# Last pass of a two-layer attention backward: V and its dS product two blocks further ahead of K, and wo read row by row

## The chip, the cores and the metric

The kernel runs on one core of a Trainium2 chip. The metric is the device time of one execution in microseconds. Three runs of the kernel before took 2030.9, 2032.97 and 2034.32 us; the median is 2032.97 us. The engines are named as in the profile: PE is TensorE (PEld are its weight loads), DVE is VectorE, ACT is ScalarE, POOL is GpSimd and SP is SyncE. A "q" behind an engine's name is its queue of DMA issues.

## The reference

A token (one row of 1024 numbers) goes through attention, a dense layer, the same attention once more and the same dense layer once more; then the gradients of everything are taken. Both attentions use one K cache and one V cache of 4 groups x 65536 rows x 128 numbers in bf16, that is 64 MiB each, and their gradients are as large.

```python
def _A_ref(x, k_cache, v_cache, wq, wo):
    q = (x @ wq).reshape(B, Sq, Hq, Dh)...        # 32 heads of 128
    k = jnp.repeat(k_cache, rep, axis=1)          # 4 groups, 8 heads each
    v = jnp.repeat(v_cache, rep, axis=1)
    scores = jnp.einsum("bhqd,bhkd->bhqk", q, k) * (Dh ** -0.5)
    o = jnp.einsum("bhqk,bhkd->bhqd", _softmax(scores, axis=-1), v)
    return o... @ wo
...
x = x + _A_ref(_layernorm(x), A_k_cache, A_v_cache, A_wq, A_wo)
x = x + _B_ref(_layernorm(x), B_w1, B_b1, B_w2, B_b2)
x = x + _A_ref(_layernorm(x), A_k_cache, A_v_cache, A_wq, A_wo)
x = x + _B_ref(_layernorm(x), B_w1, B_b1, B_w2, B_b2)
```

The outputs are the last x and the gradients of x, K, V, wq, wo, w1, b1, w2 and b2.

## The kernel before

**Four passes over K and V.** Pass 1 and pass 2 are the two forward attentions, pass 3 is the backward of the second attention and pass 4, the last, the backward of the first. Pass 4 also writes dK and dV, for both attentions at once: what a layer adds to dK and dV is an outer product of a column of the softmax and its gradient with a row of q or dO, so the 8 heads of both layers (16 rows) go into one product. Between the passes lie dense stages with w1, w2, wo and wq.

**Columns, items, blocks.** The 65536 rows of a group lie as 512 columns of 128 rows. A pipeline item is 8 columns; a block is J = 32 columns, four items, 1 MiB of K or of V. Pass 4 has 256 items, 64 blocks.

**The pipeline.** `pipeline` (L788) steps through the items; at step i a stage with lag l works on item i - l. In pass 4 (L1367) the stages are: `vT`, lag 0, transposes V on TensorE and evacuates it to `kt` (L1267); `vS`, lag 2, multiplies the transposed V by dO into one PSUM bank `ps_sc` (L1308) and, after four items, VectorE multiplies this dP by the kept exponentials E into `X` (L1316), which is dS; `dV8`, lag 3, makes dV of a block by outer products (L1329); `k8`, lag 7, multiplies K by X for dQ (L1355) and makes dK by outer products. The outer products need E and X transposed; that is `x_transpose` (L1285), of E at `vS`'s first item of a block, from a copy `xin` that POOL makes at `vT` (L1282), and of X right after X is made (L1318).

**Space.** The arena is one tile of 20 granules of 8 KiB a partition. Twelve (`NSLOT`) are for blocks of K and V, weight slabs, and staging of dV, dK and the weight gradients. The other eight are the planes of E, one for each layer and group; the planes of group g are granules 12+g and 16+g. When a group is done, its two planes become free for loads (`E_done`, L836). In pass 4 a block's granule is chosen in `take_one` (L279), and the groups run from 3 to 0. Seven blocks of V that pass 3 has turned already stay in the arena for the start of pass 4.

**Order.** Passes 1 to 3 keep the written order on PE, DVE and ACT. In pass 4 the framework's scheduler orders each engine's instructions beforehand from its own model of time; on the chip each engine then runs its list in order, and waits on semaphores. Loads are issued on SP, stores on POOL, each queue in its order. So a load whose granule is still being stored holds up the loads behind it on SP.

**Background work.** Between the items run generators, a step at a time (`Background`, L725): the projections by wq (`g_q`), by wo (`g_wo`, L859), the products of wo with the gradient (`g_dO`, L903) and wq's (`g_dn`, L930), and in pass 4 the weight gradients (`g_outer`, L1397, and `g_outer_wide`, L1416). A slab of wo for one group is 1024 x 1024, 2 MiB. In the passes it is read by `wo_runs` (L465): each partition gets eight neighbouring rows of wo, 8 or 16 KiB in one piece. Since a partition then holds other rows than the head's vector does, small matmuls with constants (`to_runs`, `from_runs`, `eighth`) turn the vector beforehand or the result afterwards. For the slabs at the ends of the passes, `wo_slabs` (L461) reads row by row: 2 KiB pieces, with the rows where the vectors have them. wq is always read in pieces of 2 KiB (`wq_slabs`, L457).

Of the kernel before, what the change touches and what calls it, by code (L numbers as in the profile page):

```python
# [10 lines left out]
BF = mybir.dt.bfloat16  # L11
# [5 lines left out]
P = 128  # L17
# [3 lines left out]
def kernel(  # L21
# [35 lines left out]
    J = 32  # L57
# [69 lines left out]

    eighth = const.tile([P, 8], F32, name="eighth")
    nc.vector.tensor_reduce(out=eighth[:], in_=ident_f[:].rearrange("p (m e) -> p e m", e=8), axis=AX.X, op=ALU.add)
    sixt = const.tile([P, 16], F32, name="sixt")  # L130
    nc.vector.tensor_reduce(out=sixt[:], in_=ident_f[:].rearrange("p (m e) -> p m e", e=8), axis=AX.X, op=ALU.add)
    to_runs = const.tile([P, 8, 16], BF, name="to_runs")
    nc.vector.tensor_copy(out=to_runs[:, :, :], in_=sixt[:, :].unsqueeze(1).to_broadcast([P, 8, 16]))
    sixt2 = const.tile([P, 16], F32, name="sixt2")
    nc.vector.tensor_reduce(out=sixt2[:], in_=ident_f[:].rearrange("p (a m) -> p m a", m=16), axis=AX.X, op=ALU.add)
    from_runs = const.tile([P, 16, 8], F32, name="from_runs")
    nc.vector.tensor_copy(out=from_runs[:, :, :], in_=sixt2[:, :].unsqueeze(2).to_broadcast([P, 16, 8]))


# [37 lines left out]
    def col_from_dram_f(v1d, n, name):  # L177
        nj = n // P
        rows = tmp.tile([nj // 4, 4 * P], BF, name="rows_f", tag="rows_f", bufs=1)
        nc.sync.dma_start(out=rows[:], in_=v1d.rearrange("(s x) -> s x", x=4 * P))  # L180
        pt = ps_mv([P, 4, 8], BF)
        col = vec.tile([P, nj // 4, 4], F32, name=name)
        for j in range(4):
            nc.tensor.transpose(pt[:, j, 0:nj // 4], f_cols(rows, j), ident_b[0:nj // 4, 0:nj // 4])
            nc.vector.tensor_copy(out=col[:, :, j], in_=pt[:, j, 0:nj // 4])
        return col[:, :, :].rearrange("p s j -> p (s j)")

    def col_to_dram_f(col, n, v1d):
        nj = n // P
        rows = tmp.tile([nj // 4, P, 4], BF, name="rows_f", tag="rows_f", bufs=1)  # L190
        c3 = col[:, :].rearrange("p (s j) -> p s j", j=4)
        for j in range(4):
            pt = ps_mv([nj // 4, P], F32)
            nc.tensor.transpose(pt[:, :], c3[:, :, j], ident_f[:, :])
            nc.vector.tensor_copy(out=rows[:, :, j], in_=pt[:])
        nc.gpsimd.dma_start(out=v1d.rearrange("(s x) -> s x", x=4 * P), in_=rows[:].rearrange("s p j -> s (p j)"))

# [188 lines left out]
    B3_LAG = TLEAD + HB // 8 + 3  # L386
    B4_LAG = TLEAD + J // 8 + 1
    DV_LAG = TLEAD + 1
    ITEMS = [order_by_unit(False, SU), order_by_unit(True, SU), order_by_unit(False, HB), order_by_unit(True, J)]
# [71 lines left out]
    def wo_slabs(g, ahead=1):  # L461
        v = rows_of(A_wo)
        return slabs("s_wo", lambda k, kn: v[:, g * R + k:g * R + k + kn, :], R, 4, 1024, ahead, True)

    def wo_runs(g):  # L465

        v = A_wo[g * 1024:(g + 1) * 1024, :].rearrange("(p k) n -> p k n", k=8)
        return slabs("s_wo", lambda k, kn: v[:, k:k + kn, :], R, 4, 1024, 1, True)[0]

# [389 lines left out]
    def g_wo(L, xacc, g, ps=ps_bg, it=None):  # L859
        def fin(p):  # L860
            nc.vector.tensor_tensor(out=xacc[:], in0=xacc[:], in1=p, op=ALU.add)
        if it is not None:
            yield from g_mv(it, R, 8, lambda kc: L["oTb"][:, g * R + kc:g * R + kc + 1], ps, fin)
            return
        each = tmp.tile([P, R, 8], BF, name="run_each", bufs=1)
        nc.vector.tensor_tensor(out=each[:, :, :], in0=L["oTb"][:, gsl(g)].unsqueeze(2).to_broadcast([P, R, 8]),
                                in1=eighth[:, :].unsqueeze(1).to_broadcast([P, R, 8]), op=ALU.mult)
        yield
        pt = ps_mv([P, R, 8])
        nc.tensor.matmul(pt[:, :, :].rearrange("p r k -> p (r k)"), lhsT=to_runs[:, :, :].rearrange("p a b -> p (a b)"),  # L870
                         rhs=each[:, :, :].rearrange("p r k -> p (r k)"), start=True, stop=True)
        yield
        own = tmp.tile([P, 8, R], F32, name="run_own", bufs=1)
        nc.vector.tensor_tensor(out=own[:, :, :], in0=pt[:, :, :].rearrange("p r k -> p k r"),
                                in1=M8[:, :].unsqueeze(1).to_broadcast([P, 8, R]), op=ALU.mult)
        oruns = tmp.tile([P, 8], F32, name="run_o")
        nc.vector.tensor_reduce(out=oruns[:], in_=own[:, :, :], axis=AX.X, op=ALU.add)
        orunb = tmp.tile([P, 8], BF, name="run_ob")
        nc.vector.tensor_copy(out=orunb[:], in_=oruns[:])
        yield  # L880
        yield from g_mv(wo_runs(g), R, 8, lambda kc: orunb[:, kc:kc + 1], ps, fin)

# [20 lines left out]
    def g_dO(L, dx, g):  # L903
        def fin(y):
            each = tmp.tile([P, R, 8], F32, name="run_own", bufs=1)
            nc.vector.tensor_tensor(out=each[:, :, :], in0=y.unsqueeze(1).to_broadcast([P, R, 8]),
                                    in1=M8[:, :].unsqueeze(2).to_broadcast([P, R, 8]), op=ALU.mult)
            yield
            pt = ps_mv([P, R, 8], F32)
            nc.tensor.matmul(pt[:, :, :].rearrange("p r k -> p (r k)"), lhsT=from_runs[:, :, :].rearrange("p a b -> p (a b)"),  # L910
                             rhs=each[:, :, :].rearrange("p r k -> p (r k)"), start=True, stop=True)
            yield
            own = tmp.tile([P, R, 8], F32, name="run_own", bufs=1)
            nc.vector.tensor_tensor(out=own[:, :, :], in0=pt[:, :, :], in1=eighth[:, :].unsqueeze(1).to_broadcast([P, R, 8]), op=ALU.mult)
            back = tmp.tile([P, R], F32, name="run_o")
            nc.vector.tensor_reduce(out=back[:], in_=own[:, :, :], axis=AX.X, op=ALU.add)
            yield
            yield from dO_finish(L, g)(back[:, :])
        yield from g_rowdots(wo_runs(g), R, dx[:], DC, fin, "%s_dO%d" % (L["name"], g))

# [17 lines left out]
    def attn_fwd(p, L, on_group, bg, end=()):  # L938
# [56 lines left out]
        def stats(g, su, S, pm):  # L995
# [23 lines left out]
            def low():  # L1019
                gm = tmp.tile([R, 1], F32, name="gm")  # L1020
                nc.vector.tensor_reduce(out=gm[:], in_=v["ptm"][:], axis=AX.X, op=ALU.min)
                v["gmb"] = tmp.tile([R, P], F32, name="gmb", bufs=1)
                nc.vector.tensor_scalar(out=v["gmb"][:], in0=ones_f[0:R, :], scalar1=gm[:, 0:1], scalar2=None, op0=ALU.mult)
# [194 lines left out]
    def attn_bwd4(p, La, Lb, on_group, bg, stack, end=()):  # L1218
# [48 lines left out]
        def vT(g, c8):  # L1267
            bg.need(g)
            vb8 = kv8("v", g, c8)
            if is_turned("v", g, c8):  # L1270
                state[("vt", g, c8)] = vb8
            else:
                pt = ps_tr()
                for i in range(8):
                    nc.tensor.transpose(pt[:, i, :], vb8[:, i, :], ident_b[:, :])  # L1275
                kv_done("v", g, c8)
                vt = turned_to("v", g, c8, vb8)
                evac(vt[:, :, :], pt[:, :, :])
                state[("vt", g, c8)] = vt
            if c8 % J == 0:  # L1280
                xin = dspool.tile([P, J, R2], BF, name="xin", tag="xin", bufs=1)
                nc.gpsimd.tensor_copy(out=split2(xin[:, :, :]), in_=E2(g, c8, J))  # L1282
                state[("xin", g, c8 // J)] = xin

# [8 lines left out]
        def vS(g, c8):  # L1293
            if c8 == gfirst[g]:
                g_setup(g)
            if c8 == sufirst[(g, c8 // SU)]:
                su_setup(g, c8 // SU)
            if c8 % J == 0:
                state[("xe", g, c8 // J)] = x_transpose(state.pop(("xin", g, c8 // J)))
            vt = state.pop(("vt", g, c8))  # L1300
# [11 lines left out]
            if (c8 + 8) % J == 0:  # L1312
                c0 = c8 + 8 - J
                ps_dp = state["ps_dp"]
                X = dspool.tile([P, J, R2], BF, name="X", tag="X")
                nc.vector.tensor_tensor(out=split2(X[:, :, :]), in0=split2(ps_dp[:, :, :]), in1=E2(g, c0, J), op=ALU.mult)  # L1316
                add_load(dve=0.13 + J * R2 * 0.00105)
                state[("xd", g, c0 // J)] = (X, x_transpose(X[:, :, :]))  # L1318
                E_done(g, c0, J)

# [22 lines left out]
        def k8(g, c8):  # L1343
            kb8 = kv8("k", g, c8)
            b, j0 = divmod(c8, J)
            su = c8 // SU
            X, xt = state[("xd", g, b)]
            if c8 == sufirst[(g, su)]:
# [17 lines left out]
        start_pass(p)  # L1366
        pipeline(items, [(vT, 0), (vS, TLEAD), (dV8, DV_LAG), (k8, B4_LAG)], bg, end)  # L1367

# [333 lines left out]
```

## Time and profile before

The profiled execution took 2032.97 us; its span from first to last instruction is 2031.2 us.

| | value |
|---|---|
| profiled execution, time | 2032.97 us |
| its span | 2031.2 us |
| PE busy / PEld / DVE / ACT / POOL | 81% / 66% / 58% / 51% / 7% |
| HBM read, written | 624.96 MB, 165.69 MB |
| mean rate over the span | 389 GB/s |
| first product of the last pass with V (L1308) | 1229.5 us |
| a load of 1 MiB of V or K, issue to landing | 15.0 and 14.6 us |
| a store of 1 MiB, issue to landing | 11.8 us |

The page has the busy share of each engine, then 40 slices of the span with the busy tenths, the granted TensorE clock and the rate of the DMA engines, then the DMA queues, the chain of work that ended last, and groups of instructions by line with what ended the idle time before them. Waits are inferred from semaphore events; where several were awaited, the last one is named. A busy TensorE includes modelled ends of its instructions, so "busy" is not "at its peak". Times in windows count from the span's start.

### The profile page before, as it was taken

What the parts mean: (1) busy time and instruction counts of PE and PEld (TensorE: products, weight loads), DVE (VectorE), ACT (ScalarE), POOL (GpSimd) and SP (SyncE); (2) the same over time, 40 slices, a digit from 0 to 9 for tenths busy, and PEclk for the clock granted to TensorE, in tenths of its full rate; (3) what the DMA queues carried; (4) which work ended last, traced back from release to release, by engine and by line L of the source; (5) the groups of instructions that cost most, each with busy time, mean ns of one, the idle gap of its engine ahead of it and who ended that gap; (6) DMA issues with size and microseconds to landing.
All of it is one profiled execution on the core that took longest, in us unless ns stands there. A gap on an engine that the chain in (4) does not pass through costs nothing. (4 is left out here: it accounts for less than half of the span.)

```text
span 2031.2 us, 67119 instructions
## 1 busy us (share of the span) xinstructions
PE 1646.9 (81%) x30228; PEld 1345.0 (66%) x30228; DVE 1178.5 (58%) x2409; ACT 1043.9 (51%) x1609; POOL 142.2 (7%) x332
## 2 busy tenths in 40 slices
PE   6877787787877877788787897798797887788996
PEld 6877777687777776777777795455455555455554
DVE  5645455345555544535454466587577676677666
ACT  3434354143443453426354265586476676567665
POOL 0000000000000000000000001111011111111111
PEclk9989999699999998988898998798699789899777
DMA  9999999989999998899999976999999999899985
GB/s 391 421 424 421 423 424 400 379 343 421 424 421 423 425 401 313 360 421 416 419 422 413 391 273 263 356 418 423 419 381 423 394 418 419 332 422 425 424 339 228
DMA packets 101006, 794.98 MB, mean 391 GB/s; under 512 B 9440, under 2 KB 9454, under 8 KB 37102
## 3 DMA queue, kind: packets, MB, share of 16 engines
q1 hardware_dynamic: 76670, 624.99, 75.1%
q0 software_dynamic: 24048, 165.70, 19.7%
q8 instruction: 236, 3.87, 0.7%
q14 instruction: 52, 0.43, 0.1%
HBM read 624.96 MB, written 165.69 MB: 389 GB/s over the span
## 5 line engine op out<-in xcount | busy, mean ns | idle before, releaser
L164 DVE COPY kt<-ps_tr 128x1024 bf16<-128x1024 bf16 x724 | 497.1, 689 | 479.6 <-PE ps_tr L962 248.4
L161 ACT CAST arena<-ps_gg 128x1024 bf16<-128x1024 f32 x454 | 443.8, 1014 | 253.3 <-PE ps_gg L1329 206.4
L962 PE MATMUL ps_tr<-ident_b,arena 128*128 128x128 bf16 x3840 | 307.7, 225 | 40.4 <-DMA arena<-in_A_k_cache_dram 27.4
L161 ACT COPY kt<-ps_tr 128x1024 bf16<-128x1024 bf16 x164 | 171.0, 1047 | 196.0 <-PE ps_tr L1154 126.3
L164 DVE CAST arena<-ps_gg 128x1024 bf16<-128x1024 f32 (+2 forms) x189 | 224.9, 1190 | 76.6 <-PE ps_gg L1329 35.3
L962 PEld LDWEIGHTS <-arena 128*128 128x128 bf16 x3840 | 232.1, 101 | 50.0 <-DMA arena<-in_A_k_cache_dram 30.3
L1064 PE MATMUL ps_acc<-arena 128*128 128x64 bf16 (+4 forms) x4096 | 206.3, 196 | 64.8 <-DMA arena<-in_A_v_cache_dram 52.5
L1329 PE MATMUL ps_gg<-GG,xt 64*128 64x512 bf16 x1024 | 215.0, 423 | 29.3 <-ACT arena L161 13.8
L1275 PE MATMUL ps_tr<-ident_b,arena 128*128 128x128 bf16 x1824 | 178.3, 238 | 36.1 <-DMA arena<-in_A_v_cache_dram 35.7
L1064 PEld LDWEIGHTS <-arena 128*128 128x128 bf16 x4096 | 160.1, 101 | 70.3 <-DMA arena<-in_A_v_cache_dram 56.5
L1045 ACT ACTIVATE arena<-S_sb,L_negm 128x128 bf16<-128x128 f32 x256 | 165.6, 1003 | 60.8 <-DVE L_negm L1030 60.8
L980 PE MATMUL ps_sc<-L_qpad,kt 128*128 128x64 bf16 (+7 forms) x3584 | 182.6, 194 | 15.2 <-issue 8.3
L1154 PE MATMUL ps_tr<-ident_b,arena 128*128 128x128 bf16 x1920 | 159.5, 230 | 42.4 <-DMA arena<-in_A_v_cache_dram 40.5
L1275 PEld LDWEIGHTS <-arena 128*128 128x128 bf16 x1824 | 121.7, 106 | 88.1 <-issue 49.0
L980 PEld LDWEIGHTS <-kt 128*128 128x128 bf16 x3584 | 152.3, 100 | 18.7 <-issue 9.0
L1154 PEld LDWEIGHTS <-arena 128*128 128x128 bf16 x1920 | 121.2, 103 | 46.6 <-DMA arena<-in_A_v_cache_dram 43.0
L1355 PE MATMUL ps_acc<-X,arena 128*128 128x64 bf16 (+3 forms) x2048 | 124.2, 200 | 18.4 <-DMA arena<-in_A_k_cache_dram 18.4
L1355 PEld LDWEIGHTS <-arena 128*128 128x128 bf16 x2048 | 88.8, 103 | 61.9 <-issue 41.7
L1045 ACT ACTIVATION_READ_ACCUMULATOR arena<-S_sb,L_negm 128x1 f32 x256 | 128.1, 500 | 0.0
L1199 PE MATMUL ps_acc<-dsT,arena 128*128 128x64 bf16 (+7 forms) x2048 | 105.8, 197 | 17.6 <-DMA arena<-in_A_k_cache_dram 14.5
L1308 PE MATMUL ps_sc<-DOB,kt 128*128 128x64 bf16 (+3 forms) x1824 | 117.2, 202 | 0.0
L1308 PEld LDWEIGHTS <-kt 128*128 128x128 bf16 x1824 | 87.5, 104 | 42.9 <-issue 41.7
(285 smaller groups left out, 2171.7 us busy)
## 6 DMA issues: line engine op xcount, KB each, us to landing
arena<-in_A_k_cache_dram SPq DMA_DIRECT2D x86, 2048.0 KB, 21.0
arena<-in_A_v_cache_dram SPq DMA_DIRECT2D x83, 2048.0 KB, 21.6
out_dram<-arena POOLq DMA_DIRECT2D x151, 1024.0 KB, 11.8
arena<-in_A_v_cache_dram SPq DMA_DIRECT2D x76, 1024.0 KB, 15.0
arena<-in_A_k_cache_dram SPq DMA_DIRECT2D x76, 1024.0 KB, 14.6
arena<-in_B_w_dram SPq DMA_DIRECT2D x32, 896.0 KB, 7.0
arena<-in_A_wo_dram SPq DMA_DIRECT2D x22, 1024.0 KB, 15.2
arena<-in_A_wq_dram SPq DMA_DIRECT2D x20, 1024.0 KB, 14.7
```

Of the source, the lines that this page charges most:

```text
L161: nc.scalar.copy(out=out, in_=in_)
L164: nc.vector.tensor_copy(out=out, in_=in_)
L962: nc.tensor.transpose(pt[:, i, :], kb8[:, i, :], ident_b[:, :])
L980: nc.tensor.matmul(state["ps_s"][:, s:s + w, :].rearrange("p a b -> p (a b)"), lhsT=kt[:, i, :], rhs=L["qpad"][:, g, 0:w, :].rearrange("p ...
L1045: nc.scalar.activation(out=E(p, g, c0, SU)[:, :, h], in_=S[:, h, :], func=ACTF.Exp, bias=L["negm"][:, g, su, h:h + 1], scale=SCALE, accum_ ...
L1064: nc.tensor.matmul(ps_o[:, 0:w, :], lhsT=vb8[:, i, :], rhs=E(p, g, c, w), start=(c % SU == 0), stop=(c % SU == SU - 1), skip_group_check=True)
L1154: nc.tensor.transpose(pt[:, i, :], vb8[:, i, :], ident_b[:, :])
L1199: nc.tensor.matmul(ps_dq[:, 0:w, :].rearrange("p a b -> p (a b)"), lhsT=kb8[:, i, :], rhs=dsT[:, s:s + w, :].rearrange("p a b -> p (a b)") ...
L1275: nc.tensor.transpose(pt[:, i, :], vb8[:, i, :], ident_b[:, :])
L1308: nc.tensor.matmul(state["ps_dp"][:, s:s + w, :].rearrange("p a b -> p (a b)"), lhsT=vt[:, i, :], rhs=DOB[:, g, 0:w, :].rearrange("p a b - ...
L1329: nc.tensor.matmul(pg[:, 512 * h:512 * h + 512], lhsT=xt[64 * h:64 * h + 64, j1 // 8 + m, :], rhs=gg[64 * h:64 * h + 64, :, :].rearrange(" ...
L1355: nc.tensor.matmul(ps_dq[:, 0:w, :].rearrange("p a b -> p (a b)"), lhsT=kb8[:, i, :], rhs=X[:, s:s + w, :].rearrange("p a b -> p (a b)"), ...
```

## The change

It has two parts.

1. In pass 4, `V_AHEAD` = 8 items (two blocks) is added to the lags of dV and of K: dV's goes from 3 to 11, K's from 7 to 15. V's transposes, dP and X keep their lags. X is no longer transposed when it is made but at K's first item of the block; X gets four buffers in place of two. The copy of E is made three steps ahead of dV (new stage `eIn`, lag 8), and transposed one step ahead of it (new stage `eT`, lag 10), which also builds the factors of the outer products (`su_setup`). The planes of E are given back by `eIn`.
2. `wo_runs` goes, with its constants and the small products around it; `g_wo` and `g_dO` read wo by `wo_slabs` inside the passes too. Two small tiles change place with it: the staging of b1 and of its gradient moves into a granule of the arena, and `gmb` gets two buffers.

```diff
-    eighth = const.tile([P, 8], F32, name="eighth")
...
-    from_runs = const.tile([P, 16, 8], F32, name="from_runs")
...
 def col_from_dram_f(v1d, n, name):
-        rows = tmp.tile([nj // 4, 4 * P], BF, name="rows_f", tag="rows_f", bufs=1)
+        sl = Slot("rows_f")
+        rows = sl.t[0:nj // 4, 0:4 * P]
...
-    B4_LAG = TLEAD + J // 8 + 1
-    DV_LAG = TLEAD + 1
+    V_AHEAD = 2 * J // 8
+    B4_LAG = TLEAD + J // 8 + 1 + V_AHEAD
+    DV_LAG = TLEAD + 1 + V_AHEAD
...
-    def wo_runs(g):
-
-        v = A_wo[g * 1024:(g + 1) * 1024, :].rearrange("(p k) n -> p k n", k=8)
-        return slabs("s_wo", lambda k, kn: v[:, k:k + kn, :], R, 4, 1024, 1, True)[0]
...
 def g_wo(L, xacc, g, ps=ps_bg, it=None):
...
-        yield from g_mv(wo_runs(g), R, 8, lambda kc: orunb[:, kc:kc + 1], ps, fin)
+        yield from g_mv(it or wo_slabs(g)[0], R, 8, lambda kc: L["oTb"][:, g * R + kc:g * R + kc + 1],
+                        ps, fin)
...
 def g_dO(L, dx, g):
...
-        yield from g_rowdots(wo_runs(g), R, dx[:], DC, fin, "%s_dO%d" % (L["name"], g))
+        yield from g_rowdots(wo_slabs(g)[0], R, dx[:], DC, dO_finish(L, g), "%s_dO%d" % (L["name"], g))
...
 def vT(g, c8):
-            if c8 % J == 0:
-                xin = dspool.tile([P, J, R2], BF, name="xin", tag="xin", bufs=1)
-                nc.gpsimd.tensor_copy(out=split2(xin[:, :, :]), in_=E2(g, c8, J))
-                state[("xin", g, c8 // J)] = xin
...
 def vS(g, c8):
-            if c8 == sufirst[(g, c8 // SU)]:
-                su_setup(g, c8 // SU)
-            if c8 % J == 0:
-                state[("xe", g, c8 // J)] = x_transpose(state.pop(("xin", g, c8 // J)))
...
-                X = dspool.tile([P, J, R2], BF, name="X", tag="X")
+                X = dspool.tile([P, J, R2], BF, name="X", tag="X", bufs=2 + V_AHEAD * 8 // J)
...
-                state[("xd", g, c0 // J)] = (X, x_transpose(X[:, :, :]))
-                E_done(g, c0, J)
+                state[("X", g, c0 // J)] = X
+
+        def eIn(g, c8):
+            if c8 % J == 0:
+                xin = dspool.tile([P, J, R2], BF, name="xin", tag="xin", bufs=1)
+                nc.gpsimd.tensor_copy(out=split2(xin[:, :, :]), in_=E2(g, c8, J))
+                state["xin"] = xin
+                E_done(g, c8, J)
+
+        def eT(g, c8):
+            if c8 == sufirst[(g, c8 // SU)]:
+                su_setup(g, c8 // SU)
+            if c8 % J == 0:
+                state[("xe", g, c8 // J)] = x_transpose(state["xin"])
...
 def k8(g, c8):
-            X, xt = state[("xd", g, b)]
+            X = state[("X", g, b)]
+            if j0 == 0:
+                state["xd"] = x_transpose(X)
+            xt = state["xd"]
...
-        pipeline(items, [(vT, 0), (vS, TLEAD), (dV8, DV_LAG), (k8, B4_LAG)], bg, end)
+        pipeline(items, [(vT, 0), (vS, TLEAD), (eIn, DV_LAG - 3), (eT, DV_LAG - 1), (dV8, DV_LAG), (k8, B4_LAG)], bg, end)
```

## Prediction

> **What bounds the kernel now.** I read the page first, then busy time by stretches, then the waits of the last pass, then single lines. The page's slices:
>
> ```profile
> PEclk9989999699999998988898998798699789899777
> DMA  9999999989999998899999976999999999899985
> GB/s 391 421 424 421 423 424 400 379 343 421 424 421 423 425 401 313 360 421 416 419 422 413 391 273 263 356 418 423 419 381 423 394 418 419 332 422 425 424 339 228
> ```
>
> Slices of 50.8 us. Wherever a pass runs undisturbed, the transfers move 421 to 425 GB/s: that is the ceiling of this kernel, and bytes missing below it are time lost. The last pass starts in slice 24 and has most of the dips. The same by stretches, last pass alone (window, length, busy us by engine, granted clock, DMA share, GB/s):
>
> ```profile
> 1240.00:1340.00 100.00, 77.80 (x913) 46.69 (x912) 62.65 (x96) 59.37 (x69) 16.54 (x32) 0.81 0.93 358
> 1340.00:1460.00 120.00, 101.16 (x1255) 64.28 (x1257) 83.51 (x154) 80.22 (x93) 18.56 (x35) 0.84 1.01 424
> 1460.00:1520.00 60.00, 51.64 (x631) 31.90 (x629) 41.57 (x68) 40.72 (x51) 11.39 (x22) 0.83 0.99 383
> 1520.00:1740.00 220.00, 171.36 (x2246) 111.22 (x2244) 151.15 (x273) 142.55 (x174) 34.97 (x66) 0.87 1.01 414
> 1740.00:1760.00 20.00, 18.91 (x232) 11.56 (x230) 16.50 (x26) 16.56 (x22) 3.35 (x6) 0.85 0.53 199
> 1760.00:1940.00 180.00, 161.53 (x2012) 100.77 (x2009) 131.32 (x226) 124.48 (x142) 34.50 (x66) 0.88 1.01 422
> 1940.00:2031.00 91.00, 72.44 (x833) 42.72 (x831) 58.16 (x112) 53.99 (x60) 13.73 (x23) 0.76 0.70 270
> ```
>
> Missing against 424 GB/s, as time: head (424-358)/424 x 100 = 15.6 us; 1460 to 1520: 5.8; 1520 to 1740: 5.2; 1740 to 1760: 10.6; 1760 to 1940: 0.8; tail (424-270)/424 x 91 = 33.1. So about 71 us of this pass are not paid for by bytes. What made the dips, from the waits (who, for whom: total, times, longest):
>
> ```profile
> SPq L341 <- DMA out_dram<-arena: 569.2, 96, 19.2
> ...
> PE ps_tr L1275 <- DMA arena<-in_A_v_cache_dram: 35.7, 9, 7.8
> PE ps_tr L1288 <- DVE X L1316: 23.3, 15, 14.2
> ...
> POOL xin L1282 <- DMA arena<-in_A_wq_dram: 17.7, 1, 17.7
> ...
> DVE X L1316 <- DMA arena<-in_A_wo_dram: 14.5, 1, 14.5
> ```
>
> Loads on SP nearly always wait for a granule that a store still holds; TensorE waits for V and for X (and 18.4 us for K). The last two lines are odd: X and its input copy read only planes of E, and yet wait for a weight slab. The built program says why: E2 takes two planes four granules apart, the slab goes into a free granule between them, and the framework's order of accesses treats the stretch as one. After each such wait the DMA share falls (1460 and 1740).
>
> **The wo read.** Twelve groups' slabs (three a pass) of 2 MiB go from eight rows a partition to single rows of 2 KB. wq is read in single rows already, so both can be measured: 36 us from the issue of a slab, wq in the first two lines (three more read 418, 420 and 419), wo in the last two.
>
> ```profile
> 75.00:111.00 36.00, 28.98 (x711) 27.69 (x710) 21.01 (x47) 18.17 (x44) 0.00 (x0) 1.00 1.01 418
> ...
> 563.00:599.00 36.00, 25.98 (x586) 24.34 (x583) 17.40 (x40) 11.54 (x25) 0.00 (x0) 0.91 1.01 418
> ...
> 108.00:144.00 36.00, 28.77 (x667) 26.87 (x663) 20.11 (x54) 14.44 (x38) 0.00 (x0) 0.95 1.01 425
> 513.00:549.00 36.00, 28.71 (x664) 27.54 (x661) 18.48 (x47) 15.73 (x38) 0.00 (x0) 0.91 1.01 425
> ```
>
> About 418.5 against 425 at the same DMA share: 6.5/425 x 36 = 0.55 us a slab. Nine lie in passes that are all DMA: 9 x 0.55 = 5.0; three in the last pass, about half of it exposed: 0.8. I take **+5.8 us** (bounds +3.3, two thirds of the nine, to +6.6). The Trainium skill, "DMA: Bandwidth & Descriptors", Specifications, gives 512 bytes as the smallest transfer at line rate, so 2 KB rows would cost nothing and the sum would be 5.8 us lower. These rows say otherwise, and the measurement is taken.
>
> What goes with it: five VectorE constants at 2 to 3.5 us (381+277+215+354+218 ns = 1.4 us, while the first slabs land) and, twelve times, about 0.9 us of small VectorE work (for dO: 220+225+220 ns) and one matmul of 0.19 to 0.29 us. All beside a DMA share of 1.0: 0 us; uncovered it would be 11 us saved at most, and only the three in the last pass (2 us) lie where an engine can bind. On SP the wo slab moves one place forward, ahead of one K load. b1 passes through a granule in place of its own tile: one 7 KB load and store, 0.
>
> **The order in the last pass.** Per block of 32 columns it issues the same 32 V transposes, 32 products with V, 32 with K, 8 transposes, 16 outer products, evacuations, two loads and two stores. Moved: V's transposes, dP and X stay; the copy of E (POOL), its transposes and su_setup go from lags 0 and 2 to 8 and 10, dV from 3 to 11, K, dQ, dK from 7 to 15; X's transposes from right after X to K's first step. On SP, a V load stands two blocks further ahead of its K; on POOL the E copy stands among later stores. In the built programs, V's products lead K's by 1.5 blocks before and about 3.5 after; in the last quarter by about 2.
>
> *X's wait.* TensorE no longer stands behind a fresh X: 23.3 us in 15 waits go, of which 14.2 is the odd wait (counted below). The 14 others are 9.1 us, worth something only where TensorE and not DMA sets the pace: 8 of the 31 stretches of 20 us from 1340 to 1960 are below 400 GB/s, so 9.1 x 0.26 = **-2.4 us** (0 to -9.1). Late next: the single dP bank, which the next block's dP may not enter before X has read it.
>
> *Head.* Seven V blocks are kept in SBUF from the pass before. V runs ahead through them without a load, so their granules come free for K sooner. Between a granule's release and its first use the built program has, for the first loads released by stores, 117 to 240 matmuls before and 203 to 299 after. TensorE's timeline has its stalls there: 7.0 us for K at 1250 and 7.8 us for V at 1278; the stretch loses 15.6. I take half, rounded: **-7 us**; bounds +5 (eleven steps before the first store, 2.0 us each as the first 28 take 56 us, with DMA idle for a quarter of them) and -15.6.
>
> *The odd waits.* Before, two cases: copy and X behind wq; X and copy behind wo. After, three: X and copy behind wq; the copy alone behind wo; copy and X behind wq once more, at three quarters. The two now stand before dips of 5.8 and 10.6 us, 8.2 on average. One more with X is +8.2; one that loses its X is half as dear, -4.1: **+4.1 us** (bounds -16.4, if X's new slack hides all, and +10.6). Queued behind X on VectorE are V's evacuations, so TensorE stops two steps later anyway; behind the copy on POOL are the stores, and SP waits for those.
>
> *Tail.* Of the last ten K loads, eight after have 89 to 295 matmuls between the store that frees their granule and their first use; in before the store-freed ones have 356 to 648. Before's blocks 54 to 63 take 117 us for some 1150 matmuls, 0.1 us each, so the leads go from 36 to 65 us down to 9 to 30. Needed is a store and a load, 11.8 + 14.6 us from the page's landing times = 26.4. Shortfalls: 7.7, 0, 0, 7, 10.1, 1.9, 9.2, 17.5 us, 53 in all if nothing hides them. Against that, V's part of 1.7 blocks leaves a tail where TensorE binds: 1.7 x 32 x (98+64 ns, busy over count at L1275 and L1308) = 8.8 us, and 33 us of missing bytes can absorb waits. A quarter of 53 less 8.8: **+4.5 us** (bounds -8.8 to +44).
>
> *Sum:* 5.8 - 2.4 - 7 + 4.1 + 4.5 = +5.0 us. The profiled execution has a time of 2032.97 us (span 2031.2 and 1.8 around it), which is also the median of the three runs. **Forecast 2038 us.**
>
> **Rivals.** *V ahead uncouples the pass (faster).* The X waits were what turned a late load into a dip, and the head fills. -9.1 (X) - 12 (head, three quarters) - 4.1 (one odd wait less dear) + 5.8 + 4.5 = -15: 2018 us. For it: 23.3 us of waits on X and the head's better leads; against: the same number of granules holds the same blocks, and single dP bank and in-order VectorE remain. It decides from the point where head and X together give over 15 us.
>
> *The tail starves (slower still).* Half of the 53 us of shortfalls is exposed: 2038 + 13 = 2051. TensorE's gaps would also lower its clock: 1720 to 1740, after the odd wait, has a granted clock of 0.64 against 0.96 before it. The Trainium skill, "TensorE: Matmul & The Clock Gate", HAM oscillation, warns that each DMA wait past the gate's window starts the next products at half clock; by it the gaps would cost more than their length.
>
> *Hidden anyway.* DMA paces the pass, the order changes nothing, and the head pays for the tail: only wo's rows are left and the last pass hides its three; in the extreme also part of the nine. 2035 us.
>
> **Chances.** Forecast 0.46, uncoupled 0.28, starved 0.14, hidden 0.12. Faster or slower by 0.2% is 4.1 us, about what a measurement of this kernel can tell from no change. Uncoupled is faster in 0.26 of its 0.28; the forecast is slower in 0.36, same in 0.07, faster in 0.03; hidden is same in 0.07, slower in 0.04, faster in 0.01; starved is slower. Together: faster 0.30, same 0.16, slower 0.54. The range reaches from 2016 (uncoupled, 2 below) to 2060 (starved with two thirds exposed), which leaves out about 1 in 6; the forecast's own range is 2029 to 2048.
>
> **What would show it.** wo: stretches around a wo slab in passes 1 to 3 at 418 instead of 425, and the start of the last pass some 5 us later. X: the wait of L1288's successor for X gone, part of it at the dP product. Head: the first 100 us of the last pass above 358 GB/s, K and V waits of 7 us gone. Odd waits: three, the last near three quarters of the pass. Tail: waits of K's product for K loads in the last 100 us, where before has none. The forecast is wrong if the middle of the pass, which I left as it is, changes by more than 10 us: every static order there is new.

## The result, and the profile after

The changed kernel takes 2042.41 us (median of four runs, 2037.85 to 2045.71), the kernel before, run beside it, 2031.93 us: a ratio of 1.0049, with an interval of 1.0027 to 1.0071. It is slower by some 10 us. The profiled execution took 2045.71 us (span 2043.9), 12.7 us more than that of before.

The page of the changed kernel, granted clock, DMA share and rate in 40 slices of 51.1 us:

```profile
PEclk9989999899999898998898998898797996978876
DMA  9999999989999998899999977999999999999974
GB/s 391 419 421 419 420 422 400 390 346 421 419 417 422 421 387 317 358 421 420 415 420 410 392 269 276 422 417 422 384 383 424 423 420 382 410 413 396 375 285 191
```

The plain stretches of passes 1 and 2 now show 417 to 422 where before had 421 to 425; in pass 3 (slices 17 to 20) the two hardly differ, 415 to 421 after and 416 to 422 before. The head of the last pass (slices 25 to 27) is better: 422, 417, 422 against 356, 418, 423. The last four slices are worse: 396, 375, 285, 191 against 425, 424, 339, 228.

To account for it, the last pass is cut in three, each time from its first product with V: 1229.5 us before, 1234.7 after. Stretches of before, then of after (window, length, busy time of PE, PEld, DVE, ACT, POOL, granted clock, DMA share, GB/s):

```profile
1229.50:1349.50 120.00, 95.28 (x1179) 57.97 (x1178) 80.19 (x133) 76.18 (x91) 20.70 (x39) 0.84 0.88 341
1349.50:1869.50 520.00, 434.05 (x5544) 277.09 (x5544) 370.53 (x653) 352.55 (x421) 87.58 (x167) 0.87 0.99 406
1869.50:2031.20 161.70, 134.78 (x1529) 79.94 (x1528) 103.05 (x189) 96.55 (x106) 27.25 (x47) 0.77 0.83 336
```

```profile
1234.70:1354.70 120.00, 105.50 (x1345) 65.45 (x1345) 87.25 (x155) 82.80 (x98) 21.22 (x40) 0.86 0.89 363
1354.70:1874.70 520.00, 427.39 (x5486) 272.38 (x5485) 359.46 (x638) 347.93 (x415) 91.28 (x168) 0.86 0.99 406
1874.70:2043.90 169.20, 127.23 (x1423) 74.72 (x1421) 101.15 (x174) 95.15 (x103) 25.74 (x46) 0.75 0.77 297
```

A stretch of t us at r GB/s lacks t x (1 - r/424). That gives 23.5, 22.1 and 33.6 us before, and 17.3, 22.1 and 50.7 us after. So the head gained 6.2 us, the middle nothing, and the tail lost 17.1. With the start of the pass, and the time that its bytes would take at 424 GB/s, this is the whole difference of the two profiled executions:

| | us |
|---|---|
| last pass starts later (1234.7 - 1229.5) | +5.2 |
| bytes already moved when it starts (its length less what it lacks: 722.5 before, 719.1 after) | -3.4 |
| head | -6.2 |
| middle | 0.0 |
| tail | +17.1 |
| sum | +12.7 |

The second row is what is left of the pass's length, so the sum has to come out; what the table tells is where the loss lies. That row can be checked by itself: both kernels move 794.98 MB in all, and in the 20 us ahead of the pass the rate is 291 GB/s before and 359 after, which is 3.2 us at 424.

Waits of the changed kernel in the last pass (who, for whom: total, times, longest):

```profile
SPq L334 <- DMA out_dram<-arena: 558.5, 98, 16.7
...
PE ps_acc L1318 <- DMA arena<-in_A_k_cache_dram: 35.6, 9, 8.1
PE ps_tr L1231 <- DMA arena<-in_A_v_cache_dram: 35.0, 10, 12.1
...
POOL xin L1271 <- DMA arena<-in_A_wq_dram: 30.8, 2, 19.1
...
DVE X L1264 <- DMA arena<-in_A_wq_dram: 21.8, 2, 16.2
...
PE ps_sc L1253 <- DVE X L1264: 20.9, 2, 16.2
```

From the loads' own queue over the last pass, and from the last 169 us alone:

```profile
SPq L429 <- DVE X L1264: 5.4, 1, 5.4
```

```profile
PE ps_acc L1318 <- DMA arena<-in_A_k_cache_dram: 19.8, 4, 8.1
```

TensorE no longer waits for X at a transpose. It waits for X at the first instruction of the next dP product (L1253), 20.9 us in two cases, and these are the odd waits: X itself stood behind a wq slab for 21.8 us. The products with K now wait 35.6 us for their loads; in the last 169 us alone it is 19.8 us in 4 waits, where before has none. POOL's timeline has the three odd waits of the copy of E, the last at three quarters of the pass (start, duration, instruction, idle time ahead of it and who ended it):

```profile
1472.32 0.62 POOL L1271 COPY xin<-arena 128x512 bf16<-128x512 bf16 x1 [19.05 <-DMA arena<-in_A_wq_dram]
...
1724.28 1.11 POOL L1271 COPY xin<-arena 128x512 bf16<-128x512 bf16 x1 [13.71 <-DMA arena<-in_A_wo_dram]
...
1833.77 0.62 POOL L1271 COPY xin<-arena 128x512 bf16<-128x512 bf16 x1 [11.75 <-DMA arena<-in_A_wq_dram]
```

Around each lies a hole in the transfers. By 20 us windows counted from the first product with V they lack 9.7, 6.5 and 3.5 us; the two of before, counted so, 5.6 and 10.8. That is 3.3 us more after, and yet the middle as a whole lacks 22.1 us in both, so the rest of it lacks that much less.

Each row below is one profiled execution, by the same cut; all kernels are described in the next section. The median is over all timed runs of a kernel. A profiled execution can lie some us off its kernel's median (V ahead with slabs apart 8.8 us above it, wo rows side by side 5.5 above, V ahead side by side 5.7 below, before with slabs apart 5.9 below), so a difference of a few us between two rows shows little.

| kernel | median | last pass starts | length | head lacks | middle | tail |
|---|---|---|---|---|---|---|
| before | 2031.9 | 1229.5 | 801.7 | 23.5 | 22.1 | 33.6 |
| after | 2042.4 | 1234.7 | 809.2 | 17.3 | 22.1 | 50.7 |
| wo rows alone | 2029.5 | 1234.9 | 793.8 | 23.8 | 20.8 | 27.2 |
| V ahead alone | 2041.5 | 1228.6 | 812.2 | 20.1 | 23.3 | 49.5 |
| before, slabs apart | 2018.1 | 1227.0 | 783.4 | 21.5 | 14.7 | 25.0 |
| after, slabs apart | 2018.1 | 1235.8 | 782.2 | 20.7 | 14.7 | 27.5 |
| V ahead, slabs apart | 2026.2 | 1233.9 | 799.3 | 20.4 | 18.4 | 40.2 |
| before, planes side by side | 2019.9 | 1231.1 | 786.4 | 23.2 | 11.0 | 30.0 |
| wo rows, side by side | 2025.0 | 1234.7 | 794.0 | 24.1 | 17.2 | 30.5 |
| V ahead, side by side | 2010.1 | 1225.1 | 777.5 | 16.4 | 14.7 | 26.9 |
| after, side by side | 2024.8 | 1235.2 | 788.8 | 18.7 | 18.4 | 32.6 |
| X late alone, side by side | 2022.6 | 1229.9 | 791.3 | 24.9 | 17.2 | 26.4 |
| V one block ahead, side by side | 2015.6 | 1232.1 | 785.2 | 23.8 | 12.3 | 26.7 |
| V ahead, lead handed back, side by side | 2014.1 | 1229.2 | 779.8 | 16.7 | 15.9 | 27.0 |

### The profile page after: what moved, and what is told of

Same layout as the page of the kernel before. It is cut to its first block, busy times and chain, and to the rows that moved or that the text cites. A ratio compares the mean times of both kernels' runs of the same rounds, so it can differ in the third digit from the quotient of the medians.

```text
span 2043.9 us, 66994 instructions
## 1 busy us (share of the span) xinstructions
PE 1635.8 (80%) x30210; PEld 1336.2 (65%) x30210; DVE 1166.6 (57%) x2364; ACT 1044.0 (51%) x1607; POOL 144.7 (7%) x332
## 2 busy tenths in 40 slices
DMA packets 110846, 794.98 MB, mean 389 GB/s; under 512 B 9425, under 2 KB 9439, under 8 KB 49375
## 5 line engine op out<-in xcount | busy, mean ns | idle before, releaser
L150 ACT CAST arena<-ps_gg 128x1024 bf16<-128x1024 f32 (+1 forms) x455 | 443.9, 1012 | 237.5 <-PE ps_gg L1289 191.7
L153 DVE CAST arena<-ps_gg 128x1024 bf16<-128x1024 f32 (+1 forms) x188 | 224.1, 1192 | 84.1 <-PE ps_gg L1289 48.2
L936 PEld LDWEIGHTS <-kt 128*128 128x128 bf16 x3584 | 152.4, 100 | 20.3 <-issue 12.7
L1318 PE MATMUL ps_acc<-X,arena 128*128 128x64 bf16 (+3 forms) x2048 | 129.9, 200 | 35.7 <-DMA arena<-in_A_k_cache_dram 35.6
L1155 PE MATMUL ps_acc<-dsT,arena 128*128 128x64 bf16 (+7 forms) x2048 | 104.3, 196 | 19.8 <-DMA arena<-in_A_k_cache_dram 15.3
## 6 DMA issues: line engine op xcount, KB each, us to landing
arena<-in_A_v_cache_dram SPq DMA_DIRECT2D x83, 2048.0 KB, 21.8
arena<-in_A_k_cache_dram SPq DMA_DIRECT2D x76, 1024.0 KB, 10.8
```

Of the source, the lines that this page charges most:

```text
L150: nc.scalar.copy(out=out, in_=in_)
L153: nc.vector.tensor_copy(out=out, in_=in_)
L936: nc.tensor.matmul(state["ps_s"][:, s:s + w, :].rearrange("p a b -> p (a b)"), lhsT=kt[:, i, :], rhs=L["qpad"][:, g, 0:w, :].rearrange("p ...
L1155: nc.tensor.matmul(ps_dq[:, 0:w, :].rearrange("p a b -> p (a b)"), lhsT=kb8[:, i, :], rhs=dsT[:, s:s + w, :].rearrange("p a b -> p (a b)") ...
L1318: nc.tensor.matmul(ps_dq[:, 0:w, :].rearrange("p a b -> p (a b)"), lhsT=kb8[:, i, :], rhs=X[:, s:s + w, :].rearrange("p a b -> p (a b)"), ...
```

## The experiments

The theory after the comparison: wo's rows cost their 5 us, running V ahead helps the head, and the tail and the holes both come from the false order between E's planes and the granules that lie between them. The rival: running V ahead makes K late by itself, and the odd waits are an accident beside it.

### Each part of the change alone

Kernel before, wo by rows:

```diff
 def g_wo(L, xacc, g, ps=ps_bg, it=None):
...
-        yield from g_mv(wo_runs(g), R, 8, lambda kc: orunb[:, kc:kc + 1], ps, fin)
+        yield from g_mv(wo_slabs(g)[0], R, 8, lambda kc: L["oTb"][:, g * R + kc:g * R + kc + 1], ps, fin)
...
 def g_dO(L, dx, g):
...
-        yield from g_rowdots(wo_runs(g), R, dx[:], DC, fin, "%s_dO%d" % (L["name"], g))
+        yield from g_rowdots(wo_slabs(g)[0], R, dx[:], DC, dO_finish(L, g), "%s_dO%d" % (L["name"], g))
```

> The kernel before with one part of the change: wo is read by single rows, the order of the last pass stays. Theory (rows of 2 KB cost 0.55 us a slab): the last pass starts about 5 us later than the 1229.5 us of before, as after the whole change (1234.7). Rival (the later start came from somewhere else, rows cost nothing): it starts at 1229.5. The small edit also moves the weight slabs to other granules, and in the built program only one odd wait is left (the copy of E behind wo; the two of before stood in front of 5.8 and 11 us of missing bytes). So the total by the theory is 2032 + 5.5 less 6 to 12 for the odd wait that goes = 2026 to 2032; by the rival 2020 to 2026.

Measured: 2029.5 us, ratio 0.9988 (0.9974 to 1.0002), last pass from 1234.9 us. The later start is there without the other part of the change, and the total is where the theory had it, though not by the way that the theory named: against before the middle gains only 1.3 us and the tail 6.4. Windows of 36 us around wo slabs, this kernel first, then V ahead alone, which reads wo by runs, in the same three places:

```profile
106.00:142.00 36.00, 26.61 (x580) 24.88 (x576) 16.85 (x44) 10.22 (x23) 0.00 (x0) 0.84 1.01 418
509.00:545.00 36.00, 28.15 (x681) 27.09 (x679) 17.77 (x41) 16.70 (x42) 0.00 (x0) 0.91 1.01 419
602.00:638.00 36.00, 25.81 (x588) 24.85 (x584) 15.08 (x37) 13.89 (x35) 0.00 (x0) 0.86 1.01 419
```

```profile
106.00:142.00 36.00, 29.46 (x724) 27.73 (x722) 21.08 (x55) 13.19 (x33) 0.00 (x0) 1.00 1.01 424
509.00:545.00 36.00, 28.20 (x644) 27.07 (x642) 17.85 (x45) 16.85 (x42) 0.00 (x0) 0.91 1.01 424
602.00:638.00 36.00, 28.90 (x691) 27.48 (x687) 19.42 (x49) 16.95 (x40) 0.00 (x0) 0.95 1.01 423
```

The DMA share is full in both, and the rows move 5 GB/s less. In pass 3 single windows don't tell the two apart: around its two wo slabs the four kernels with rows, with planes apart and side by side, show 414 to 419 GB/s, the four with runs 416 to 425. The kernel before has 416 and 421 there (from 926 and 1016 us), and the prediction, which puts wo by runs at 425, shows only the two windows from passes 1 and 2.

The total did not rise with the start. This small edit also put the weight slabs of the last pass in other granules: in its trace neither X nor the copy waits for a slab, where the built program had led to expect one such wait, and the tail lacks 27.2 us in place of 33.6. That the second follows from the first is likely, but not shown.

Kernel after, wo by runs again (the small tiles of the runs share one scratch tile):

```diff
-        yield from g_mv(it or wo_slabs(g)[0], R, 8, lambda kc: L["oTb"][:, g * R + kc:g * R + kc + 1],
-                        ps, fin)
...
+        yield from g_mv(wo_runs(g), R, 8, lambda kc: orunb[:, kc:kc + 1], ps, fin)
...
-                v["gmb"] = tmp.tile([R, P], F32, name="gmb")
+                v["gmb"] = tmp.tile([R, P], F32, name="gmb", bufs=1)
...
-            cf = tmp.tile([P, 2, R2], F32, name="cf")
+            cf = tmp.tile([P, 2, R2], F32, name="cf", bufs=1)
...
-                CC8 = tmp.tile([P, 8, R2], BF, name="CC8")
+                CC8 = tmp.tile([P, 8, R2], BF, name="CC8", bufs=1)
```

> The other part of the change alone: V two blocks ahead, X transposed late, wo still read by eight-row runs (three small scratch tiles have one buffer instead of two to make room). Theory by the ledger of missing bytes in the last pass: start as before (1229.5); head 9 us better; middle 4 us better; one odd wait (copy only) in place of two, 10 to 13 us better; the last 100 us about 18 us worse as K loads come late: 2032 - 9 - 4 - 12 + 18 = 2025. Rival (running V ahead is what costs, wherever the odd waits fall): 2042 - 5 = 2037.

Measured: 2041.5 us, ratio 1.0045 (1.0027 to 1.0063). The theory's 2025 is out: V ahead alone is 10 us slower than before, with its head better by 3.4 us, its tail worse by 16, and its middle no better (23.3 us against 22.1) although it has one odd wait in place of two. This spoke for the rival. Two of its waits in the last pass:

```profile
POOL xin L1321 <- DMA arena<-in_A_wq_dram: 22.9, 1, 22.9
...
DVE mv_t L571 <- DMA arena<-in_A_wq_dram: 16.5, 1, 16.5
```

The transfers lack 9.3 us there. Not only the copy waits for the slab, its own reader on VectorE (mv_t) does too: the slab is late, and the hole can't all be put down to the copy. A later hole of 7.1 us, from 1809 to 1849 us, has no odd wait beside it; there the products with K wait 11.9 us for their loads. A load into a granule between two planes has to wait for the reads of E that stand before it in the program; in the changed kernel SP waits 5.4 us for X ahead of a slab. So false order can make such a load late at its issue, and then make the next reads of E wait for its landing. In V ahead alone the slabs' loads waited on SP almost only for stores (39.4 us), so what made that slab late is not shown.

### Slabs kept apart

```diff
-    def take_one(fill, load=False):
+    def take_one(fill, load=False, apart=False):
         by_age = sorted((t, i) for i, t in FREE.items())
+        if apart:
+            by_age = [x for x in by_age if not 12 < x[1] < 19] or by_age
...
-            self.i = take_one(fill, load) if at is None else at
+            self.i = take_one(fill, load, PS["pass4"] and name in ("s_wq", "s_wo")) if at is None else at
```

> The changed kernel with one thing more: in the last pass weight slabs take no granule that lies between two planes of E, so that none of the three odd waits is there. Theory (each odd wait leaves a hole in the transfers that is never filled; the three holes are 9.8, 6.8 and 4 us of missing bytes): 2042 - 17 to 21 = 2021 to 2025. Rival (the time comes back in the tail, where late K loads set the end anyway): 2037 or more.

Measured: 2018.1 us, ratio 0.9926 (0.9907 to 0.9945): 24 us off the changed kernel and below what was expected. The middle accounts for 7.4 us of it (22.1 to 14.7) and the tail for 23.2 (50.7 to 27.5), while the head gives 3.4 back. So the theory was right about the total only: the three holes had lacked 19.7 us, and though neither X nor the copy waits for a load any more, two other holes, of 6.3 and 4.0 us, stand in the middle. What makes those stayed open. The rival, that late K loads set the end anyway, is out for this kernel.

> The kernel before with the same rule for weight slabs, so that its two odd waits are gone. Theory: the holes of 5.8 and 11 us go, 2032 - 14 to 17 = 2015 to 2018. Rival (the end is set by the work of the tail): 2028 or more.

Measured: 2018.1 us, ratio 0.9921 (0.9894 to 0.9949), as expected in total. Here too the middle gains 7.4 us, not the 16.4 of the two holes, and the tail 8.6. With the slabs apart, the changed kernel and the one before take the same time, although the changed one still pays for the rows of wo.

### Planes side by side

The planes of group g move from granules 12+g and 16+g to 12+2g and 13+2g, so that nothing lies between them, for slabs and for K and V:

```diff
     def plane(lay, g):
-        return NSLOT + G * lay + g
+        return NSLOT + 2 * g + lay
...
-    EALL = ARENA[:, NSLOT * BLK:].rearrange("p (l g c r) -> p l g c r", l=2, g=G, r=R)
+    EALL = ARENA[:, NSLOT * BLK:].rearrange("p (g l c r) -> p l g c r", l=2, g=G, r=R)
```

The same edit was made in four kernels: before, after, and each part alone.

> The kernel before with the two planes of E of a group put side by side in the arena, in place of four granules apart; what reads them then spans nothing but these two, so that no load of any kind stands between. Theory (the false order is behind the holes of the last pass): as with weight slabs kept apart, 2015 to 2018, or a few us less, the last pass about 780 long. Rival (what was gained with slabs apart came from the other granules that the loads got, not from the order): 2028 or more. Open: in the first two passes fewer pairs of granules are free, so the last pass may start at another time than 1228.

Measured: 2019.9 us, ratio 0.9940 (0.9925 to 0.9955): nearly the gain of the slabs apart. In this kernel nothing beyond the slabs shows.

> The changed kernel with the two planes side by side. In the built program the last K loads of the pass now have 220 to 450 matmuls between the release of their granule and their use, where the changed kernel has 89 to 295 and some below nothing. Theory (holes and short leads of the changed kernel both come from the false order): last pass about 775 long, total 1235 + 775 + 2 = 2012. Rival A (V ahead makes K loads late by itself): tail still near 50 us of missing bytes, total 2030 or more. Rival B (slabs were all there was to it): 2018, as with slabs apart.

Measured: 2024.8 us, ratio 0.9952 (0.9933 to 0.9971), between the theory's 2012 and rival A's 2030, and no better than with slabs apart. The tail lacks 32.6 us where the changed kernel lacks 50.7: rival A is out. Rival B is the nearest, so in this kernel too nothing beyond the slabs shows. And with the planes side by side the whole change is still no gain: 2024.8 against the 2019.9 of the kernel before.

> V ahead alone (wo by eight-row runs) with the planes side by side. Theory: as the changed kernel with planes side by side, less the 6 to 7 us of single wo rows: 2005, and 5 to 9 us below the kernel before with planes side by side, by the head of the pass and X's waits. Rival (V ahead costs by itself, as its 2041.5 alone suggested): 5 us or more above the kernel before with planes side by side.

Measured: 2010.1 us, ratio 0.9893 (0.9872 to 0.9913). This is 5 us above the theory's 2005, and the fastest of all, 1.1% below the kernel before and 1.6% below the changed one, and the rival that V ahead costs by itself falls here: the very same stages took 2041.5 with the planes apart. Its stretches, with the planes apart first and then side by side:

```profile
1228.60:1348.60 120.00, 102.17 (x1301) 63.62 (x1301) 83.80 (x147) 79.75 (x95) 21.04 (x40) 0.84 0.88 353
1348.60:1868.60 520.00, 425.99 (x5520) 272.77 (x5518) 361.59 (x639) 348.88 (x420) 89.97 (x167) 0.87 0.99 405
1868.60:2040.80 172.20, 129.12 (x1439) 75.53 (x1436) 102.91 (x187) 95.83 (x105) 27.75 (x49) 0.76 0.78 302
```

```profile
1225.10:1345.10 120.00, 102.84 (x1343) 64.47 (x1342) 86.78 (x154) 82.38 (x98) 21.88 (x42) 0.89 0.91 366
1345.10:1865.10 520.00, 440.76 (x5646) 281.47 (x5645) 373.70 (x651) 358.56 (x429) 93.87 (x174) 0.86 1.00 412
1865.10:2002.60 137.50, 106.96 (x1273) 64.89 (x1269) 90.07 (x167) 84.42 (x92) 23.26 (x40) 0.81 0.85 341
```

The tail goes from 302 to 341 GB/s and from 172 to 138 us. In it the products with K waited for their loads 18.5 us in 5 waits with the planes apart; with the planes side by side there is no such wait.

> Wo by single rows in the kernel before, with the planes side by side: the read alone, with no odd wait in either of the two kernels compared. Theory (0.55 us a slab and more): 5.5 to 7 us above the kernel before with planes side by side, and the last pass starts that much later. Rival (rows of 2 KB cost nothing; the start differs by where weight slabs are put): within 2 us.

Measured: 2025.0 us, ratio 0.9959 (0.9943 to 0.9975): 5.2 us above the kernel before with the same planes, just below what was expected; the intervals of the two overlap. The last pass starts 3.6 us later than there. Over all kernels the last pass starts at 1234.7 to 1235.8 us where wo is read by rows (five of them, mean 1235.1) and at 1225.1 to 1233.9 where it is read by runs (nine, mean 1229.6): 5.5 us. This mean is the firmest measure of the rows; single starts of kernels with runs differ by up to 8.8 us.

With the planes side by side the four medians are 2019.9 (neither part), 2025.0 (rows), 2010.1 (V ahead), 2024.8 (both). The parts don't add: both together cost 9.5 us more than their sum, which is only just clear of noise, as the runs of one kernel spread over 8 to 15 us. Nor are the parts quite alike: in V ahead alone the small tiles `cf` and `CC8` have one buffer, in the other three kernels two. The profile of both lacks more in the middle than V ahead alone (18.4 against 14.7), and starts its last pass 10 us later; why it is more than the rows' 5 us was not settled.

### What is left of running V ahead

> V ahead alone with E's planes four granules apart as before, and only the weight slabs kept out from between them; K and V loads still go there. In the built program five of the last fourteen K loads then stand behind a read of E that their granule is not part of, with 41, -74, -130, 1 and -4 matmuls or so between that read and their use. Theory (K loads pay for the false order too, in the tail): the slab's hole of 9 us goes, the tail of 50 us of missing bytes stays, 2028 to 2034. Rival (slabs were the whole of it): 2010, as with the planes side by side.

The edit is the one shown for slabs apart. Measured: 2026.2 us, ratio 0.9979 (0.9965 to 0.9993), a little below what was expected and 16 us above the planes side by side. In this kernel, then, the slabs were not the whole of it, and K and V loads pay for the false order too, as far as the other granules that they get are not behind it. In the tail the products with K wait 10.5 us for their loads, between 18.5 (nothing done) and none (planes side by side). The tail lacks 40.2 us, between 49.5 and 26.9, but in a profiled execution of 2035.0 us, the slowest of twelve.

X transposed when its K arrives, nothing else moved (kernel before with the planes side by side):

```diff
-                state[("xd", g, c0 // J)] = (X, x_transpose(X[:, :, :]))
+                state[("xd", g, c0 // J)] = X
...
-            X, xt = state[("xd", g, b)]
+            X = state[("xd", g, b)]
+            if j0 == 0:
+                state["xdT"] = x_transpose(X[:, :, :])
+            xt = state["xdT"]
```

> The kernel before with planes side by side and one step of the change: X is transposed when its K arrives; V, the copy of E and dV stay where they were. Theory (TensorE's waits for X lie beside transfers): 0 to 3 us below the 2019.9 of the kernel before with planes side by side. Rival (X's transposes are what V ahead gains): about 2010.

Measured: 2022.6 us, ratio 0.9952 (0.9934 to 0.9970), against 0.9940 without the step. No gain can be seen. It had little to win: in the kernel that it was made from, TensorE waits for X only 5.4 us in 18 times.

V's steps paused for two blocks in the last group (V ahead, planes side by side; a plane of E is given back when X and the copy have both read it):

```diff
+        def v_at(lag):
+            def k_of(i):
+                k = i - lag
+                if k < 200:
+                    return k
+                return k - V_AHEAD if k >= 200 + V_AHEAD else None
+            return k_of
...
-        pipeline(items, [(vT, 0), (vS, TLEAD), (eIn, DV_LAG - 3), (eT, DV_LAG - 1), (dV8, DV_LAG), (k8, B4_LAG)], bg, end)
+        pipeline(items, [(vT, v_at(0)), (vS, v_at(TLEAD)), (eIn, DV_LAG - 3), (eT, DV_LAG - 1), (dV8, DV_LAG), (k8, B4_LAG)], bg, end)
```

> V ahead alone with planes side by side; in the last group of K and V heads, 14 blocks before the end, V's steps pause for two blocks, so that K's loads again come 1.5 blocks behind V's to the end, as in the kernel before. In the built program the last K loads then have 380 to 496 matmuls of lead against 269 to 468. Theory (once nothing stands behind E, the lead of V costs the tail nothing): 2008 to 2013 against 2010. Rival (the tail still pays for V ahead): 2000 to 2005.

Measured: 2014.1 us, ratio 0.9919 (0.9900 to 0.9939), a little above the theory and 9 us above the rival. The tail lacks 27.0 us as against 26.9: giving the lead back wins nothing, so no cost of the lead in the tail can be seen.

One block in place of two:

```diff
-    V_AHEAD = 2 * J // 8
+    V_AHEAD = J // 8
```

> V ahead by one block in place of two, with planes side by side and wo by eight-row runs. Theory (the head gains because kept V blocks free granules for K; one block gives about half): 2013 to 2016, between 2019.9 without and 2010.1 with two blocks. Rival (all that counts is that X is not waited for, one block does that): 2010. If the gain of V ahead is a lucky static order, anything from 2005 to 2025.

Measured: 2015.6 us, ratio 0.9924 (0.9902 to 0.9947), near half the gain of two blocks, as expected in size, though 4 us are at the edge of what these runs can tell. The place is not the expected one: its head lacks 23.8 us, as without any lead.

## Why the prediction was right, and where it was not

The forecast was 2038 us and slower; measured were 2042.4, slower, inside the range. That it came so near is in part luck: the tail was 12.6 us worse than its term, and the bytes moved ahead of the pass (3.4) and a middle that did not change (forecast +1.7 for X and the odd waits together) took some of it back. Step by step:

- **The wo read, +5.8 us: right.** The last pass starts 5.2 us later, 5.5 us in the mean over fourteen kernels, and alone, side by side, it costs 5.2 us on the medians. The windows shown for it were the clearer ones; those of pass 3 don't separate rows and runs. The Trainium skill, "DMA: Bandwidth & Descriptors", Specifications, taken by itself, would have made rows of 2 KB free, being far above its 512 bytes; these runs disagree, with 418 to 419 GB/s against 423 to 424 at the same DMA share.
- **X's wait, -2.4 us: not seen.** The wait moved to the dP product as foretold. Transposing X late, by itself, gave 2.7 us more, not less, within what these runs can tell from nothing. So no part of the waits is seen to have counted, not even the 26% that I took.
- **Head, -7 us: right in size, its reason only in part.** -6.2 us, with 3.4 us of bytes more moved before the pass starts. V's wait of 7.8 us in the first 100 us is gone (1.8 left); K's total of 9.4 us is 9.1, so "granules come free for K sooner" does not show; it is V that no longer waits. The gain is not the same everywhere: against the kernel with the same wo read and the same placing it is 1.1 to 6.8 us for two blocks, and none for one block.
- **The odd waits, +4.1 us: the sum nearly right, one step in it wrong.** There are three, the last near three quarters of the pass, and their holes lack 19.7 us against 16.4, +3.3. But "one that loses its X is half as dear" is not borne out: the copy alone stood before holes of 6.5 us, and of 9.3 us in V ahead alone. Stores are queued behind it on POOL and loads wait for those; and in both the slab was late for its own reader too, which may be part of the price. Nor is a hole a cost by itself: the middle lacks 22.1 us in both kernels, and with the slabs apart less than half of what the holes had lacked was won there.
- **Tail, +4.5 us: mis-sized, it is +17.1.** This is the step that failed. I took a quarter of the 53 us of shortfalls as exposed, less 8.8 for work that still lay ahead; half of it, as in the rival "the tail starves", gives 26.5 - 8.8 = 17.7. The rival's total of 2051, 18 us more than before against 12.7 in the profiles, was still too high, mainly by the 3.4 us of bytes that were moved ahead of the pass, for which there was no term.
- **Why the leads were short: wrong.** I read the leads of 89 to 295 matmuls as what running V ahead does to K. With the same lags and the planes side by side they are 220 to 448, and the tail lacks 32.6 us in place of 50.7; giving K's lead back to the end wins nothing (2014.1 against 2010.1). Before calling short leads the price of the order, I had found the false order and used it for the slabs alone; K and V loads go through the same granules. Which loads it was differs by kernel: in the changed one, keeping the slabs alone apart already took the tail to 27.5 us, and in V ahead alone it did not.

On the other rivals: "V ahead uncouples the pass" (2018) was no empty thought. With the planes side by side V ahead alone is 9.8 us faster than the kernel before. Of the 14.8 us between those two profiled executions, the head gives 6.8 and the tail 3.1, the middle takes 3.7 back, 2.7 are bytes already moved when the pass begins, and 6.0 are its earlier start, which differs as much among kernels with the same wo read. "Hidden anyway" fell with the tail. The Trainium skill's warning of gaps that lower TensorE's clock ("TensorE: Matmul & The Clock Gate", HAM oscillation) can add little to the difference here: the granted clock of the tail is 0.75 after and 0.77 before. No run takes it apart from the gaps themselves.

What stays open: why both parts together, side by side, are 9.5 us above the sum of the parts; what makes the holes that are left with no odd wait beside them; and how much of a tail is a K load held by a read of E, and how much the other granules that loads get once some are kept free, since no kernel changed the one without the other.

## What to carry to other kernels

When an instruction reads two places with one access pattern, ask what lies between them: a framework that orders accesses by their span makes everything there wait, in both directions. A wait of an engine for a transfer that it doesn't read is worth following to the address before anything is costed; here moving two planes together was worth more than the change under study, and turned the sign of its larger part. A reordering whose effect was measured on top of such a defect says little about the reordering.

## What the runs showed that was not expected

- Placing mattered more than order here: the same stages took 2041.5 and 2010.1 us with E's planes four granules apart and side by side.
- Pieces of 2 KB are slower than pieces of 8 or 16 KB at a full DMA share, about 419 against 424 GB/s for reads from HBM in passes 1 and 2.
- An edit that has nothing to do with the last pass (wo by rows in the kernel before) left none of its two odd waits and made its tail 6 us better; in the built program the weight slabs had come to lie in other granules.
